# A new order for the first loads and products of a gated attention and token-MLP kernel

## The chip, the cores and the metric

One core of a Trainium2 chip. The metric is the device time of one execution in microseconds (us).

## The reference

The input `x` is 2048 tokens by 512 columns (bfloat16). Two branches are mixed by a gate per token. `a` is attention with 32 heads of 16, where each token sees eight tokens (itself and every second one before it). `b` is an MLP across tokens.

```python
g = sigmoid((x * gate_w).sum(-1, keepdims=True))
# a: sliding dilated attention
q, k, v = split(x @ wqkv)                 # 512 -> 3 x 512, 32 heads of 16
idx = pos[:, None] - 2 * arange(8)        # masked where idx < 0
o = softmax((q . k[idx]) / 4) @ v[idx]
a = o @ wo
# b: token MLP
h = layernorm(x)
u = gelu(einsum("bsd,sf->bdf", h, w1) + b1)   # 2048 tokens -> 1792
b = (einsum("bdf,fs->bds", u, w2) + b2).T     # 1792 -> 2048 tokens
return g * a + (1 - g) * b
```

## The kernel before

The kernel writes down operations with their reads, writes and an estimated duration. A small planner in the same file sorts them into one program per engine: on each engine it takes what can start first by its own estimates, and it sets the semaphores. `after` and the lists given to `chain` fix the order where the author wanted it. On the chip every engine runs its list strictly in order.

Tokens are handled in four blocks of 512. `XT` holds x transposed (columns on partitions, in four slices `dt` of 128 columns), `X` the tokens as they are, for the layernorm and the MLP. A projection (`f_proj`, the matmul at line 619) is four products of 128x128 weights with 128x512 of `XT`, one per slice, summed in one of eight PSUM banks. `tn` is 0, 1 or 2 for q, k and v, `dl` a quarter of their columns, `sb` the block.

**The start.** TensorE runs filler products on constants (`f_warm`, line 537) until data are there. SP first loads the first 128 columns of block 0 as they are (`XP`, `d_xp`). TensorE turns them with the identity (`f_tr`, line 545) into banks 5 and 6; ScalarE copies one half (line 555) and VectorE the other (line 557) into `XT`. The other 384 columns of block 0 come by a transposing DMA (`ld_xt0`, line 473). The first two slices of Wq are loaded on ScalarE's queue. On SP follow, after the transposing DMA, two slices of Wq, four of Wk, x 0 and 1, and block 1's transposing DMA (`ld_xt(1)`, line 460). Later loads wait for an earlier one, five back in the list `init_dmas` (`throttle`). Wv comes in one load of 512 KB behind all blocks of x.

The first 32 real products are q and k of block 0 for all `dl`, in the eight banks, slice by slice as the data come:

```python
for (b0, d0, d1, s0, s1) in ((0, 0, 1, 0, 512), (0, 1, 2, 0, 512), (0, 2, 3, 0, 512),
                             (0, 3, 4, 0, 512), (4, 0, 2, 0, 512), (4, 2, 4, 0, 512)):
    for b in range(b0, b0 + 4):
```

After them comes `seq_proj`: q and k of block 1, q and k of blocks 2 and 3, then v of all blocks. Each group of four products goes to the next of banks 0 to 3, and ScalarE copies it out (lines 627 for q, 630 for k and v).

**What follows.** VectorE forms q times shifted k (`qkm`, line 690): eight half-length products for the first four window positions, four full ones for the rest. TensorE sums them over heads in a burst of 64 products per half (`qkr`, line 698). The softmax, the sums with v (lines 797 to 802) and the layernorm statistics (`ln1`, line 574) are VectorE's too; its order is one long `chain`. The MLP's products are at line 812 (first, followed by the gelu on ScalarE, line 833) and 862 (second, followed by line 930). The output projection is at line 878 and the final mix on VectorE at line 899.

Of the kernel before, what the change touches and what calls it, by code (L numbers as in the profile page):

```python
# [5 lines left out]
BF16 = mybir.dt.bfloat16  # L6
# [3 lines left out]
AF = mybir.ActivationFunctionType  # L10
# [3 lines left out]
D = 512  # L14
# [319 lines left out]
def bass_gated_mix__sliding_local_dilated__mixer_token_mlp__prompt_kernel(nc, A_x, A_wqkv, A_wo, B_x, B_w1, B_b1, B_w2, B_b2, gate_w, out, dbg=None):  # L334
    with contextlib.ExitStack() as es:
        view, pview, off, total = _views(nc, es)
        ps = es.enter_context(nc.psum_tensor("ps", [128, 8, 512], FP32))
        esem = {e: es.enter_context(nc.semaphore("sem_" + e)) for e in ("pool", "act", "dve", "pe")}
        sch = _Sched()

        x2d = A_x[0]
        xv = x2d.rearrange("(t p) d -> p t d", p=128)
        wqkv_v = A_wqkv.rearrange("(dt p) c -> p dt c", p=128)
# [25 lines left out]
        IDENT = view("IDENT", BF16, [(1, 128)])  # L369
# [45 lines left out]
        A = sch.add  # L415
# [12 lines left out]
        def mk_dma(dst, src):  # L428
            return lambda e: e.dma_start(dst, src)

        init_dmas = []
# [4 lines left out]
        def prev_dma():  # L436
            return [init_dmas[-1]] if init_dmas else []

        def ld_x(t0, n, q="sp"):
            ds = sch.dsem("x%d" % t0)  # L440
            op = sch.dma(q, mk_dma(X[:, t0:t0 + n, :], xv[:, t0:t0 + n, :]), n * 128 * D * 2, ds,
                         writes=["x%d" % t for t in range(t0, t0 + n)], deps=throttle() if q == "sp" else [], after=prev_dma() if q == "sp" else [], name="d_x%d" % t0)
            if q == "sp":
                init_dmas.append(op)
            return op

        def ld_w(tn, d0, n, q="sp"):
            ds = sch.dsem("wqkv%d_%d" % (tn, d0))
            op = sch.dma(q, mk_dma(WQKV[:, d0:d0 + n, tn * D:(tn + 1) * D], wqkv_v[:, d0:d0 + n, tn * D:(tn + 1) * D]),
                         n * 128 * D * 2, ds, writes=["wqkv%d_%d" % (tn, dt) for dt in range(d0, d0 + n)],  # L450
                         deps=throttle() if q == "sp" and n == 4 else [], after=prev_dma() if q == "sp" else [],
                         issue=0.65 if n == 4 else 0.45, name="d_wp%d_%d" % (tn, d0))
            if q == "sp":
                init_dmas.append(op)
            return op
# [5 lines left out]
                         writes=["xt_%d" % t for t in range(4 * sb, 4 * sb + 4)], deps=throttle(), after=prev_dma(), name="d_xt%d" % sb)  # L461
            init_dmas.append(op)

        XT0 = ["xt0_%d" % d for d in range(4)] + ["xt0_0b"]
        ALLXT = XT0 + ["xt_%d" % t for t in range(4, NST)]

        def xt_of(sb, d0=0, d1=4):
            return XT0[d0:d1] + (XT0[4:] if d0 == 0 else []) if sb == 0 else ["xt_%d" % t for t in range(4 * sb, 4 * sb + 4)]

        def ld_xt0():  # L470
            ds = sch.dsem("xt0")
            dst = XT[:, 1:4, 0:512]
            op = sch.dma("sp", lambda e: e.dma_start_transpose(dst, x2d[0:512, 128:512]), 512 * 384 * 2, ds, issue=1.25,
                         writes=XT0[1:4], after=prev_dma(), name="d_xt0")
            init_dmas.append(op)
            return op

        XP = view("OUTS", BF16, [(128, 4), (1, 128)])
        d_xp = sch.dma("sp", mk_dma(XP, xv[:, 0:4, 0:128]), 512 * 128 * 2, sch.dsem("xp"), writes=["outs0"], issue=0.4, name="d_xp")
        d_xp.lands = 3.9  # L480
        init_dmas.append(d_xp)

        first_loads = [ld_w(0, 0, 1, "act"), ld_xt0(), ld_w(0, 1, 1, "act"), ld_w(0, 2, 1), ld_w(0, 3, 1), ld_w(1, 0, 2), ld_w(1, 2, 2),
                       ld_x(0, 2)]
        ld_xt(1)
        first_loads.append(init_dmas[-1])
        for op_, t_ in zip(first_loads, (3.5, 5.7, 5.0, 6.3, 6.7, 7.6, 8.6, 9.4, 11.0)):
            op_.lands = t_
            op_.deps.clear()
        first_loads[2].order.add(first_loads[0])  # L490
        init_dmas[:] = [first_loads[1]] + first_loads[5:]
        ld_x(2, 2)
        ld_x(4, 4)
        ld_xt(2)
        ld_xt(3)
        ld_x(8, 4)
        ld_x(12, 4)
        ld_w(2, 0, 4)
        d_w1 = []

        def ld_w1(j):
# [4 lines left out]
            if j < 4:  # L506
# [8 lines left out]
                       writes=["wo"], deps=throttle(), after=prev_dma(), name="d_wo")  # L515
# [25 lines left out]
        def f_tr(h):  # L541
            def fn(e):
                ins = None
                for t in range(2):
                    ins = e.matmul(ps[:, 5 + h, 128 * t:128 * t + 128], lhsT=XP[:, 2 * h + t, :], rhs=IDENT, start=True, stop=True)  # L545
# [5 lines left out]
        ta_ = A("pe", f_tr(0), 0.215, reads=["outs0", "ident"], writes=["lg5_0", "lg5_1"], after=[w2_], name="tr0", prio=-100)  # L551
        tr_ = A("pe", f_tr(1), 0.215, reads=["outs0", "ident"], writes=["lg6_0", "lg6_1"], after=[ta_], name="tr1", prio=-100)
        A("pe", f_warm(1), 0.43, writes=["lg7_0", "lg7_1"], after=[tr_], name="warm3", prio=-100)
        w3_ = tr_
        A("act", lambda e: e.activation(out=XT[:, 0, 0:256], in_=ps[:, 5, 0:256], func=AF.Copy), 0.35, reads=["lg5_0", "lg5_1"],
          writes=["xt0_0"], name="ev_tra", prio=0)
        A("dve", lambda e: e.tensor_copy(out=XT[:, 0, 256:512], in_=ps[:, 6, 0:256]), 0.35, reads=["lg6_0", "lg6_1"],  # L557
          writes=["xt0_0b"], name="ev_trb", prio=0)

        JK = view("OUTS", BF16, [(1, D)], extra=0)  # L560
        def cols(v_, lo, n, step=1):
# [45 lines left out]
        last_main = [None]  # L607
# [37 lines left out]
        seq_proj = []  # L645
        for dl in range(4):
            seq_proj += [(0, dl, 1), (1, dl, 1)]
        for dl in range(4):
            seq_proj += [(0, dl, 2), (0, dl, 3), (1, dl, 2), (1, dl, 3)]
        for dl in range(4):  # L650
            seq_proj += [(2, dl, sb) for sb in range(4)]
        for (tn, dl, sb) in seq_proj:
            xr = xt_of(sb)
            bank = main_bank()
# [1 line left out]
                             reads=xr + ["wqkv%d_%d" % (tn, dt) for dt in range(4)],  # L656
                             writes=["acc%d" % bank], after=[last_main[0]], name="pj_%s%d_%d" % (tnames[tn], dl, sb), prio=0)
# [395 lines left out]
```

## Time and profile before

| | |
|---|---|
| median of 3 runs | 168.34 us (168.12 to 168.81) |
| profiled execution | 168.55 us, span 167.3 us |
| TensorE busy (PE) | 163.9 us, 98% |
| VectorE busy (DVE) | 151.3 us, 90% |
| ScalarE busy (ACT) | 75.0 us, 45% |
| DMA | 29.64 MB, mean 177 GB/s |
| granted TensorE clock | 1.00 |

PE is the matmul part of TensorE and PEld its weight loads, which overlap the matmuls. A row of the timeline gives start, duration, engine, line, operation, shape and count; in square brackets stands how long the engine was idle before it, and what ended that. SPq and ACTq are the queues' issuing instructions. "us to landing" runs from the issue of a DMA until its semaphore is complete. The span leaves out 1.25 us of the profiled execution that lie around it.

### The profile page before, as it was taken

How to read it: one execution, taken by the hardware profiler on the slowest of the kernel's cores; microseconds unless marked ns; L12 is line 12 of the kernel's file. 1: busy time of each engine (PE TensorE's matmuls, PEld its weight loads, DVE VectorE, ACT ScalarE, POOL GpSimd, SP SyncE). 2: the span in 40 equal slices, each digit the busy share in tenths (PEclk: the TensorE clock that was granted, in tenths of full speed). 3: DMA queues.
4: the chain of work that ended last, by engine and by line, in shares of the span. 5: the costliest groups of instructions: out<-in, count | busy, mean ns of one | idle time of the engine just before them, and what ended most of it. 6: DMA issues, size and time to landing. Idle time of an engine off the chain costs nothing.

```text
span 167.3 us, 2152 instructions
## 1 busy us (share of the span) xinstructions
PE 163.9 (98%) x860; PEld 77.6 (46%) x860; DVE 151.3 (90%) x154; ACT 75.0 (45%) x116; POOL 0.7 (0%) x8
## 2 busy tenths in 40 slices
PE   7999999999999999999999999999999999999994
PEld 2455555554454444444444444444444444444463
DVE  0145999999999999999999999999999999999896
ACT  3077688889899818793113121131231321310100
POOL 1000000000000000000000000000000000000000
DMA  5999999968003837996579936462672580000454
GB/s 130 315 272 262 303 322 291 307 196 246 0 0 97 311 115 187 303 290 153 133 183 343 335 129 143 112 187 68 184 218 83 138 223 0 0 0 0 157 190 159
DMA packets 47625, 29.64 MB, mean 177 GB/s; under 512 B 9856, under 2 KB 46464, under 8 KB 47616
## 3 DMA queue, kind: packets, MB, share of 16 engines
q1 hardware_dynamic: 45504, 24.85, 54.0%
q10 hardware_dynamic: 2112, 4.66, 10.0%
q8 instruction: 7, 0.11, 0.3%
q14 instruction: 2, 0.02, 0.0%
HBM read 21.24 MB, written 2.10 MB: 140 GB/s over the span
## 4 chain that ended last, share of the span: by engine, by line
PE 94%; DVE 3%; DMA 2%; issue 0%
PE ps L812 29%; PE ps L862 29%; PE ps L619 25%; PE ps L878 6%; PE ps L698 4%; DVE arena L899 2%; DMA arena<-in_A_x_dram 2%; PE ps L545 0%; DVE arena L557 0%
## 5 line engine op out<-in xcount | busy, mean ns | idle before, releaser
L812 PE MATMUL ps<-arena 128*128 128x512 bf16 x224 | 48.7, 379 | 0.0
L862 PE MATMUL ps<-arena 128*128 128x512 bf16 x224 | 48.7, 379 | 0.0
L619 PE MATMUL ps<-arena 128*128 128x512 bf16 x192 | 42.3, 382 | 0.1
L690 DVE TENSOR_TENSOR arena<-arena 128x4096 bf16<-128x4096 bf16 (+1 forms) x12 | 35.5, 2996 | 2.3 <-ACT arena L630 1.8
L797 DVE TENSOR_TENSOR arena<-arena 128x8192 bf16<-128x8192 bf16 x8 | 35.0, 4419 | 0.0
L812 PEld LDWEIGHTS ps<-arena 128*128 128x128 bf16 x224 | 21.8, 98 | 26.7 <-ACT arena L728 0.4
L862 PEld LDWEIGHTS ps<-arena 128*128 128x128 bf16 x224 | 21.9, 98 | 26.5
L619 PEld LDWEIGHTS ps<-arena 128*128 128x128 bf16 x192 | 21.6, 114 | 20.8 <-DVE arena L557 0.7
L930 ACT ACTIVATE arena<-ps,arena 128x512 bf16<-128x512 f32 x16 | 12.4, 778 | 39.4 <-PE ps L862 39.4
L800 DVE TENSOR_TENSOR arena<-arena 128x4096 bf16<-128x4096 bf16 (+1 forms) x16 | 27.0, 1752 | 0.0
L630 ACT ACTIVATE arena<-ps 128x512 bf16<-128x512 f32 x32 | 18.5, 596 | 4.5 <-PE ps L619 4.5
L833 ACT ACTIVATE arena<-ps,arena 128x512 bf16<-128x512 f32 x14 | 9.6, 687 | 22.2 <-PE ps L812 17.4
L574 DVE BATCH_NORM_STATS2 arena<-arena 128x6 f32<-128x512 bf16 x16 | 10.0, 680 | 5.6 <-DMA arena<-in_A_x_dram 5.6
L878 PE MATMUL ps<-arena 128*128 128x512 bf16 (+1 forms) x80 | 14.2, 337 | 0.0
L899 DVE SCALAR_TENSOR_TENSOR arena<-ps,arena 128x512 bf16<-128x512 f32 (+1 forms) x20 | 11.5, 638 | 0.9 <-PE ps L878 0.7
L598 ACT ACTIVATE arena<-arena 128x512 bf16<-128x512 bf16 x16 | 12.2, 806 | 0.0
L627 ACT ACTIVATE arena<-ps 128x512 bf16<-128x512 f32 x16 | 9.0, 596 | 5.5 <-PE ps L619 5.4
L878 PEld LDWEIGHTS ps<-arena 128*128 128x128 bf16 x80 | 7.8, 98 | 6.3
L674 DVE SCALAR_TENSOR_TENSOR arena<-arena 128x512 bf16<-128x512 bf16 x16 | 10.1, 685 | 0.0
L744 DVE TENSOR_TENSOR arena<-arena 128x512 bf16<-128x512 bf16 (+4 forms) x11 | 7.3, 667 | 0.6 <-ACT arena L763 0.2
L698 PE MATMUL ps<-arena 128*32 128x512 bf16 x128 | 7.3, 380 | 0.0
L728 ACT ACTIVATE arena<-ps 128x512 bf16<-128x512 f32 x8 | 4.7, 592 | 4.6 <-PE ps L698 4.6
(42 smaller groups left out, 40.5 us busy)
## 6 DMA issues: line engine op xcount, KB each, us to landing
arena<-in_B_w_dram SPq DMA_DIRECT2D x7, 1024.0 KB, 8.3
arena<-in_B_w_dram SPq DMA_DIRECT2D x8, 896.0 KB, 5.1
arena<-arena ACTq DMA_DIRECT2D x32, 128.0 KB, 3.0
arena<-in_A_x_dram SPq DMA_DIRECT2D x4, 512.0 KB, 5.1
out_dram<-arena SPq DMA_DIRECT2D x14, 128.0 KB, 1.7
arena<-in_A_x_dram SPq DMA_DIRECT2D x1, 1536.0 KB, 7.9
arena<-in_A_wqkv_dram SPq DMA_DIRECT2D x2, 256.0 KB, 3.6
arena<-in_A_x_dram SPq DMA_DIRECT2D x2, 256.0 KB, 3.5
```

Of the source, the lines that this page charges most:

```text
L598: A("act", (lambda t_: (lambda e: e.activation(out=X[:, t_, :], in_=X[:, t_, :], func=AF.Identity, scale=col(RSTD, t_), bias=col(NMR, t_)) ...
L619: ins = e.matmul(ps[:, bank, s0:s1], lhsT=lhsT, rhs=XT[:, dt, sb * 512 + s0:sb * 512 + s1], start=(dt == 0 and s0 == 0), stop=(dt == 3))
L630: return lambda e: e.activation(out=dst, in_=ps[:, bank, :], func=AF.Copy)
L690: return lambda e: e.tensor_tensor(out=PBL[buf][:, :, 512 * c0:512 * (c0 + nc_)], in0=in0, in1=in1, op=ALU.mult)
L698: ins = e.matmul(ps[32 * c:32 * c + 32, 4 + wl, :], lhsT=RP, rhs=PBL[buf][:, wl, c * 512:(c + 1) * 512], start=(dl == 0), stop=(dl == 3), ...
L797: A("dve", (lambda o_, i0, i1: (lambda e: e.tensor_tensor(out=o_, in0=i0, in1=i1, op=ALU.mult)))(pv, in0, in1), 4.4, reads=v_res + ["atx_% ...
L800: A("dve", (lambda pv_, n__: (lambda e: e.tensor_tensor(out=pv_[:, 0:n__], in0=pv_[:, 0:n__], in1=pv_[:, n__:2 * n__], op=ALU.add)))(pv, n ...
L812: ins = e.matmul(ps[:, bank, :], lhsT=W1W[:, slot, st, 128 * e_:128 * e_ + 128], rhs=X[:, st, :], start=(st == 0), stop=(st == NST - 1))
L862: ins = e.matmul(ps[:, bank, :], lhsT=W2S[slot][:, ft, 128 * e_:128 * e_ + 128], rhs=UT[:, ft, :], start=(ft == 0), stop=(ft == NFT - 1))
L878: ins = e.matmul(ps[:, bank, 0:c1 - c0], lhsT=OT[:, t, 128 * i:128 * i + 128], rhs=WO[:, t, c0:c1], start=(t == 0), stop=(t == 3))
L899: A("dve", (lambda i_, b_, c0_, c1_: (lambda e: e.scalar_tensor_tensor(out=T1[:, i_, c0_:c1_], in0=ps[:, b_, 0:c1_ - c0_], scalar=col(G, i ...
L930: A("act", (lambda i_, bank_: (lambda e: e.activation(out=T1[:, i_, :], in_=ps[:, bank_, :], func=AF.Identity, scale=col(OMG, i_), bias=co ...
```

## The change

- Block 0's first 256 columns, not 128, come as they are: two loads on SP (`ld_xp(0)`, `ld_xp(1)`), each turned by four TensorE products (`turn(0)`, `turn(1)`) and copied by ScalarE and VectorE. The transposing DMA (`ld_xt0`) brings the other 256 columns.
- All first loads are on SP, in one line: columns 0 to 127, Wq slice 0, Wk slice 0, columns 128 to 255, q and k weights of slice 1 in one load (`ld_qk`), the transposing DMA, q and k weights of slices 2 and 3, the whole of Wv, x 0 and 1, then block 1's transposing DMA.
- The filler before the first turn is one product shorter; a half-width one is added after it.
- The first 32 products go q slice 0, the second turn, k slice 0 (banks 4, 7, 5, 6), q and k slice 1, q slice 2, q slice 3, k slices 2 and 3.
- Eight products of v, `dl` 0 and 1 of block 0, stand in front of q and k of block 1.
- In VectorE's chain the copies of both turns come first, and `ln1` 4 and 5 move ahead of the first `qkm`.
- `init_dmas`, the list that later loads throttle on, now starts at the load of slice 2's weights.

```diff
-        XT0 = ["xt0_%d" % d for d in range(4)] + ["xt0_0b"]
+        XT0 = ["xt0_%d" % d for d in range(4)] + ["xt0_0b", "xt0_1b"]
...
-            dst = XT[:, 1:4, 0:512]
-            op = sch.dma("sp", lambda e: e.dma_start_transpose(dst, x2d[0:512, 128:512]), 512 * 384 * 2, ds, issue=1.25,
-                         writes=XT0[1:4], after=prev_dma(), name="d_xt0")
+            dst = XT[:, 2:4, 0:512]
+            op = sch.dma("sp", lambda e: e.dma_start_transpose(dst, x2d[0:512, 256:512]), 512 * 256 * 2, ds, issue=1.25,
+                         writes=XT0[2:4], after=prev_dma(), name="d_xt0")
...
-        XP = view("OUTS", BF16, [(128, 4), (1, 128)])
-        d_xp = sch.dma("sp", mk_dma(XP, xv[:, 0:4, 0:128]), 512 * 128 * 2, sch.dsem("xp"), writes=["outs0"], issue=0.4, name="d_xp")
-        d_xp.lands = 3.9
-        init_dmas.append(d_xp)
-
-        first_loads = [ld_w(0, 0, 1, "act"), ld_xt0(), ld_w(0, 1, 1, "act"), ld_w(0, 2, 1), ld_w(0, 3, 1), ld_w(1, 0, 2), ld_w(1, 2, 2),
-                       ld_x(0, 2)]
+        XP = view("OUTS", BF16, [(512, 2), (128, 4), (1, 128)])
+
+        def ld_xp(dt):
+            op = sch.dma("sp", mk_dma(XP[:, dt], xv[:, 0:4, 128 * dt:128 * dt + 128]), 512 * 128 * 2, sch.dsem("xp%d" % dt),
+                         writes=["outs%d" % dt], after=prev_dma(), issue=0.4, name="d_xp%d" % dt)
...
+        def ld_qk(d):
+            ds = sch.dsem("wqk%d" % d)
+            op = sch.dma("sp", mk_dma(WQKV[:, d, 0:2 * D], wqkv_v[:, d, 0:2 * D]), 2 * 128 * D * 2, ds,
+                         writes=["wqkv0_%d" % d, "wqkv1_%d" % d], after=prev_dma(), issue=0.45, name="d_wqk%d" % d)
...
+        first_loads = [ld_xp(0), ld_w(0, 0, 1), ld_w(1, 0, 1), ld_xp(1), ld_qk(1), ld_xt0(), ld_qk(2), ld_qk(3), ld_w(2, 0, 4), ld_x(0, 2)]
         ld_xt(1)
         first_loads.append(init_dmas[-1])
-        for op_, t_ in zip(first_loads, (3.5, 5.7, 5.0, 6.3, 6.7, 7.6, 8.6, 9.4, 11.0)):
+        for op_, t_ in zip(first_loads, (3.1, 3.8, 4.3, 4.7, 5.8, 7.2, 7.9, 8.6, 10.2, 10.9, 12.8)):
             op_.lands = t_
             op_.deps.clear()
-        first_loads[2].order.add(first_loads[0])
-        init_dmas[:] = [first_loads[1]] + first_loads[5:]
+        init_dmas[:] = first_loads[6:]
...
-        ld_w(2, 0, 4)
...
+        def turn(dt, prev):
+            for h in range(2):
+                lgr = ["lg%d_0" % (5 + h), "lg%d_1" % (5 + h)]
+                prev = A("pe", f_tr(dt, h), 0.215 if dt == 0 else 0.11, reads=["outs%d" % dt, "ident"], writes=lgr, after=[prev],
+                         name="tr%d%d" % (dt, h), prio=-100 if dt == 0 else 0)
...
-        A("pe", f_warm(6), 2.56, writes=["lg7_0", "lg7_1"], name="warm1", prio=-100)
+        A("pe", f_warm(5), 2.13, writes=["lg7_0", "lg7_1"], name="warm1", prio=-100)
         w2_ = A("pe", f_warm(1, 256), 0.2, writes=["lg7_0", "lg7_1"], name="warm2", prio=-100)
...
+        tr_ = turn(0, w2_)
         A("pe", f_warm(1), 0.43, writes=["lg7_0", "lg7_1"], after=[tr_], name="warm3", prio=-100)
...
+        w3_ = A("pe", f_warm(1, 256), 0.2, writes=["lg7_0", "lg7_1"], after=[tr_], name="warm4", prio=-100)
...
-        for (b0, d0, d1, s0, s1) in ((0, 0, 1, 0, 512), (0, 1, 2, 0, 512), (0, 2, 3, 0, 512), (0, 3, 4, 0, 512), (4, 0, 2, 0, 512), (4, 2, 4, 0, 512)):
-            for b in range(b0, b0 + 4):
+        for (bs, d0, d1, s0, s1) in ((range(4), 0, 1, 0, 512), ((4, 7, 5, 6), 0, 1, 0, 512), (range(8), 1, 2, 0, 512),
+                                     (range(4), 2, 3, 0, 512), (range(4), 3, 4, 0, 512), (range(4, 8), 2, 4, 0, 512)):
+            if bs == (4, 7, 5, 6):
+                last_main[0] = turn(1, last_main[0])
+            for b in bs:
...
-        seq_proj = []
+        seq_proj = [(2, dl, 0) for dl in range(2)]
         for dl in range(4):
             seq_proj += [(0, dl, 1), (1, dl, 1)]
...
-            seq_proj += [(2, dl, sb) for sb in range(4)]
+            seq_proj += [(2, dl, sb) for sb in range(1 if dl < 2 else 0, 4)]
...
-        chain(["rp", "ev_trb"] + ln1(0, 1, 2, 3) + ["qkm_0_0_0", "qkm_0_1_0"] + ln1(4, 5, 6, 7) + ln2(0)
+        chain(["rp", "ev_trb0", "ev_trb1"] + ln1(*range(6)) + ["qkm_0_0_0", "qkm_0_1_0"] + ln1(6, 7) + ln2(0)
```

More of the change, by code (lines that the diff above doesn't have):

```diff
@@ L462, in ld_xt @@
             init_dmas.append(op)
-        XT0 = ["xt0_%d" % d for d in range(4)] + ["xt0_0b"]
+        XT0 = ["xt0_%d" % d for d in range(4)] + ["xt0_0b", "xt0_1b"]
         ALLXT = XT0 + ["xt_%d" % t for t in range(4, NST)]
         def xt_of(sb, d0=0, d1=4):
-            return XT0[d0:d1] + (XT0[4:] if d0 == 0 else []) if sb == 0 else ["xt_%d" % t for t in range(4 * sb, 4 * sb + 4)]
+            return XT0[d0:d1] + XT0[4 + d0:4 + d1] if sb == 0 else ["xt_%d" % t for t in range(4 * sb, 4 * sb + 4)]
@@ new lines, in ld_xp @@
+        def ld_xp(dt):
+            op = sch.dma("sp", mk_dma(XP[:, dt], xv[:, 0:4, 128 * dt:128 * dt + 128]), 512 * 128 * 2, sch.dsem("xp%d" % dt),
+                         writes=["outs%d" % dt], after=prev_dma(), issue=0.4, name="d_xp%d" % dt)
+            init_dmas.append(op)
+            return op
+        def ld_qk(d):
+            ds = sch.dsem("wqk%d" % d)
+            op = sch.dma("sp", mk_dma(WQKV[:, d, 0:2 * D], wqkv_v[:, d, 0:2 * D]), 2 * 128 * D * 2, ds,
+                         writes=["wqkv0_%d" % d, "wqkv1_%d" % d], after=prev_dma(), issue=0.45, name="d_wqk%d" % d)
+            init_dmas.append(op)
+            return op
@@ L539, in f_warm, with f_tr @@
             return fn
-        def f_tr(h):
+        def f_tr(dt, h):
             def fn(e):
@@ L544, in fn @@
                 for t in range(2):
-                    ins = e.matmul(ps[:, 5 + h, 128 * t:128 * t + 128], lhsT=XP[:, 2 * h + t, :], rhs=IDENT, start=True, stop=True)
+                    ins = e.matmul(ps[:, 5 + h, 128 * t:128 * t + 128], lhsT=XP[:, dt, 2 * h + t, :], rhs=IDENT, start=True, stop=True)
                 return ins
             return fn
-        A("pe", f_warm(6), 2.56, writes=["lg7_0", "lg7_1"], name="warm1", prio=-100)
+        def turn(dt, prev):
[3 more added lines that the diff above has]
+                         name="tr%d%d" % (dt, h), prio=-100 if dt == 0 else 0)
+                dst = XT[:, dt, 256 * h:256 * h + 256]
+                pin = ps[:, 5 + h, 0:256]
+                if h == 0:
+                    A("act", (lambda d_, i_: (lambda e: e.activation(out=d_, in_=i_, func=AF.Copy)))(dst, pin), 0.35,
+                      reads=lgr, writes=["xt0_%d" % dt], name="ev_tra%d" % dt, prio=0)
+                else:
+                    A("dve", (lambda d_, i_: (lambda e: e.tensor_copy(out=d_, in_=i_)))(dst, pin), 0.35,
+                      reads=lgr, writes=["xt0_%db" % dt], name="ev_trb%d" % dt, prio=0)
+            return prev
@@ L550, in bass_gated_mix__sliding_local_dilated__mixer_token_mlp__prompt_kernel @@
+        A("pe", f_warm(5), 2.13, writes=["lg7_0", "lg7_1"], name="warm1", prio=-100)
         w2_ = A("pe", f_warm(1, 256), 0.2, writes=["lg7_0", "lg7_1"], name="warm2", prio=-100)
-        ta_ = A("pe", f_tr(0), 0.215, reads=["outs0", "ident"], writes=["lg5_0", "lg5_1"], after=[w2_], name="tr0", prio=-100)
-        tr_ = A("pe", f_tr(1), 0.215, reads=["outs0", "ident"], writes=["lg6_0", "lg6_1"], after=[ta_], name="tr1", prio=-100)
+        tr_ = turn(0, w2_)
         A("pe", f_warm(1), 0.43, writes=["lg7_0", "lg7_1"], after=[tr_], name="warm3", prio=-100)
-        w3_ = tr_
@@ L555, in bass_gated_mix__sliding_local_dilated__mixer_token_mlp__prompt_kernel @@
[L555 to L558, printed above, removed]
+        w3_ = A("pe", f_warm(1, 256), 0.2, writes=["lg7_0", "lg7_1"], after=[tr_], name="warm4", prio=-100)
         JK = view("OUTS", BF16, [(1, D)], extra=0)
```

## The prediction

> **What bounds the kernel now.** I read the page's busy times first, then the chain of waits in order of time, then the timeline of the first 22 us, and last the two places where VectorE and TensorE meet.
>
> ```profile
> PE 163.9 (98%) x860; PEld 77.6 (46%) x860; DVE 151.3 (90%) x154; ACT 75.0 (45%) x116; POOL 0.7 (0%) x8
> ```
>
> TensorE has work in 98% of the span, VectorE in 90%. A change to the loads can move the end only through these two engines.
>
> ```profile
> 0.80 3.10 DMA arena<-in_A_x_dram
> 3.91 0.14 issue
> 4.04 0.60 PE ps L545 x4
> 4.64 0.02 issue
> 4.66 0.44 DVE arena L557
> 5.10 0.05 issue
> 5.15 33.44 PE ps L619 x152
> ```
>
> This is the head of the chain of waits. The first load (128 columns of block 0, issued at 0.80) lands at 3.91; TensorE turns it (L545), VectorE copies it (L557), and the first real product starts at 5.15. From there the chain stays on TensorE until 161.65 with no wait between its pieces. So the saving is what the head saves, less what TensorE gets to do on top, unless a new wait opens later.
>
> ```profile
> 5.14 0.15 PEld L619 LDWEIGHTS ps<-arena 128*128 128x128 bf16 x2 [0.68 <-DVE arena L557]
> 5.56 0.15 PEld L619 LDWEIGHTS ps<-arena 128*128 128x128 bf16 x1 [0.27 <-issue]
> 5.98 15.93 PEld L619 LDWEIGHTS ps<-arena 128*128 128x128 bf16 x74 [0.28 <-issue]
> ```
>
> The timeline of the start shows the pace. Weight loads follow the products: 5.14, 5.56, 5.98 is one product per 0.42 us; then 74 in 15.93 us, 0.215 each. The warm-up products before (L537) also step by 0.43. So TensorE runs at half pace until about 6.1, though the granted clock reads 1.00 in this stretch, and three of the real products pay for it: (6.1 - 5.15)/2 = 0.48 us lost.
>
> ```profile
> 15.08 4.49 DVE L690 TENSOR_TENSOR arena<-arena 128x4096 bf16<-128x4096 bf16 x2 [1.84 <-ACT arena L630]
> ...
> 42.20 4.43 DVE L690 TENSOR_TENSOR arena<-arena 128x8192 bf16<-128x8192 bf16 x1 [0.41 <-PE ps L698]
> ```
>
> ```profile
> 157.36 8.29 DVE L899 SCALAR_TENSOR_TENSOR arena<-ps,arena 128x512 bf16<-128x512 f32 x15 [0.72 <-PE ps L878]
> ```
>
> VectorE starts its long chain at 15.08 and then waits for TensorE only in places: 0.41 us at 42.2, 0.72 at 157.36. These are its reserve; a later start costs nothing until they are used up.
>
> **The head, step by step.** Times are of the profiled execution (span 167.3, 168.55 in all, 0.21 above the median 168.34); a difference found there is put on the median.
>
> First load. It keeps its place at 0.80 on SP, but ScalarE's two weight loads (128 KB each, issued 0.80 to 1.82) no longer share the DMA engines with it. At worst it lands at 3.91 as now; at best those 256 KB at some 350 GB/s, the fastest fortieths of the first 12 us, go from ahead of it: 3.91 - 0.75 = 3.16. I take 3.3, nearer the best, because the two loads lie wholly in its time now. Wq's first slice, now second on SP, issues at 1.29 (today's spacing 0.49) and lands 3.0 later, the row of such loads: 4.3. Turning follows landing by 0.13 and the first product follows turning by 1.11 (4.04 to 5.15), so the product starts at 3.3 + 0.13 + 1.11 = 4.54 (4.4 to 5.15). The filler after the turn (four turns 0.43, one wide 0.43, one half 0.21) frees TensorE at 4.50, and Wq is there. Saved: 0.60.
>
> Half pace. If it still ends at 6.1, products now lie under it for 1.56 us and lose 0.78 instead of 0.48: 0.30 given back.
>
> Second turn. Four new 128-column products: 0.107 each at half pace (0.43 in the row of L545 from start to start), 0.055 at full: 0.22 to 0.43. The four products of q ahead take 1.71 at half pace, to 6.2, so I take 0.22. Its data, fourth on SP, issues at 2.3 and lands by 5.4 with today's 3.1: hidden. Banks 5 and 6 are wanted back by k: ScalarE copies in 0.38, VectorE in 0.42, each some 0.2 behind the turn, while TensorE has two k products (0.43) and the second turn itself as cover: 0.1 of wait, at most 0.4.
>
> Sum of the head: -0.60 + 0.30 + 0.22 + 0.10 = +0.02. With the ends of the unknowns, -0.4 to +0.6. The 33rd product, 12.52 now (5.15, three steps to 6.26, 29 of 0.216), stays there.
>
> The pages give a rule against the 256-byte runs: the Trainium skill, "DMA: Bandwidth & Descriptors", Specifications, asks for at least 512 B per transfer for line rate. Here 128 KB in such runs took 3.1 us to land and 128 KB in runs of 1 KB 3.0, so I follow the rows; at half rate the loads behind would come some 0.4 later each, still ahead of their use.
>
> **Behind the head.** The SP order moves: ten loads now stand before block 1's transposing DMA, Wv's 512 KB among them, where seven did on SP. Its issue moves from 5.58 to about 6.4: 0.80, nine plain loads at 0.49, and the smaller transposing one (1.64 x 2/3 = 1.1). At 280 GB/s 512 KB are 1.8 us. Block 1 landed 5.5 us after issue, the median of the three transposing loads of the first 12 us, at 11.0; now 11.0 + 0.9 at least and 11.0 + 0.9 + 1.8 = 13.7 at most. The eight v products end at 12.5 + 8 x 0.216 = 14.2. Those are the cover: no wait, but a margin of only 0.5 at the upper end. Wv itself stands before x 0 and 1, which landed at 9.05, and so lands near 10, before 12.5. x 4 to 7 land at 13.7 now (issue at 9.5, 4.2 to landing), then at 15.5, or 16.4 with the issue delay. ScalarE's issues vanish from 0.80 to 1.82; its table load (1.28) only comes sooner. Nothing there is late.
>
> VectorE. Its first product needs q and k of block 1: 12.5 + 16 x 0.216 + 0.83 (14.25 to 15.08 now) = 16.8, 1.7 later. Two of the bn_stats (0.6 each) go ahead of it, if x 4 has landed by 15.5, and fill 1.2. So VectorE is 0.5 late. The last of its first eight products (L690, start 35.08) then waits for the last k copy, which is 1.73 later too: on ScalarE two such copies ended at 34.90, so 35.8 to 36.6, and the lag there is 0.7 to 1.5. At 42.2 VectorE waits 0.41 for L698's TensorE burst today; that much is absorbed, 0.3 to 1.1 remain. At the softmax the lag reaches ScalarE:
>
> ```profile
> 73.63 2.25 ACT L833 ACTIVATE arena<-ps,arena 128x512 bf16<-128x512 f32 x3
> ```
>
> The first of these three gelus (0.69) frees at 74.32 the bank that the seventh group of the MLP's first product takes at 64.77 + 3 x 3.455 = 75.14. Reserve 0.82. At 157.36 there are 0.72 and some tenths after. A lag up to 0.8 is free, then TensorE stands; I take 0.05 for this. The burst of L698 began at 38.5. The last k product ends at 12.52 + 24 groups of 0.864 = 33.25 now and 1.73 later then, 35.0; four groups are left to 38.5, just enough for copy (0.6), product (2.28) and two hand-overs; 0 to 0.3.
>
> Total: between -0.3 and +0.4 for the likeliest values. The end of half pace need not be at 6.1 in all executions; averaged over earlier ends (below) the head is -0.2, and with 0.05 for VectorE I put -0.15 on the median: 168.2.
>
> **Rivals.**
> The clock, faster. If half pace ended before the first product, today's 0.48 goes and the head saves 0.60 - 0.32 = 0.28: 168.55 - 0.76 = 167.8, and 167.5 with the first load at 3.1. For it: after the turn TensorE stands still for some 0.3 us before 5.15, and the new order fills that; the runs spread from 168.12 to 168.81, about such a stretch. Against: 2.9 us of unbroken warm-up from 0.84 did not end it by 5.1. If it lasts to 7.5 instead, 0.78 becomes 1.48: 169.3. The rule behind it is in the Trainium skill, "TensorE: Matmul & The Clock Gate", Part 1: the window is free-running and about 3.4 us, so an identical kernel meets it at different places. The half pace of the trace agrees; its place in time was seen in one execution only.
>
> Block 1 late, slower. In-order TensorE stands at q of block 1 from 14.2 on, one for one. Landing at 15.1 decides; if Wv's delay is paid twice, once on the SP issue (a transposing load holds SP 3.2 to 3.5 us when the queue is full) and once on the bytes, it lands at 15.3: +1.1, 169.3. For it: the DMA share is over 0.9 in every stretch of 2 us from 2 to 16. Against: 1.4 us beyond my upper end.
>
> VectorE late, slower. A lag of 1.8 at 65 us makes the gelu 1.0 late: 169.3. It needs x 4 to 7 at 17 or L698 two groups later; the 0.41 and 0.82 stand against it.
>
> The eight products of v could also wait for Wv; it would have to land after 12.6, 2.6 late, and I count this with block 1.
>
> **How the numbers follow.** Forecast 0.62 at 168.2 (own range 167.8 to 168.8); clock 0.18, mostly early, about half of it over the bound; block 1 late 0.08; VectorE late 0.12. A difference within 0.5% (0.84 us) is about what a measurement of this kernel cannot tell from none. Faster needs under 167.5: 0.10 from the clock and 0.02 from the forecast. Slower needs over 169.18: most of the two slow rivals and a tail of the forecast and a late clock, 0.18. Same 0.70. Range 167.6 to 169.2.
>
> **What would show it.** First product near 4.5; its step 0.42 until about 6.1; L545 twice with four products; the 33rd product near 12.5; no TensorE wait near 14.2; VectorE's L690 at 16.8 and its wait at 42.2 shorter; TensorE unbroken at 75.1. I am wrong if the first load lands at 3.9, if the half pace ends elsewhere, or if a row of TensorE shows a wait after 12.5.

## The result and the profile after

| | before | after |
|---|---|---|
| median of 22 runs | 168.43 us (167.91 to 168.90) | 169.20 us (168.19 to 170.81) |
| profiled execution | 168.55 us, span 167.3 | 169.48 us, span 168.2 |

The ratio is 1.0042 (95% interval 1.0025 to 1.0058): slower by 0.4%, clear of the noise. The forecast was 168.2, a little faster than before; the median stands at the upper end of the forecast's range, on the other side. One execution of the changed kernel (170.81) was in a slow state and is not in the ratio; without it the runs after still scatter more than twice as wide (168.19 to 170.50).

The chain of waits of the changed kernel, in order of time (start, duration, what), from block 0's transposing DMA on; before these rows it runs over SP's five earlier issues:

```profile
3.34 1.29 SPq L473
4.63 0.05 issue
4.68 0.58 SPq L429
5.26 0.04 issue
5.30 5.39 DMA arena<-in_A_wqkv_dram
10.69 0.05 issue
10.74 29.55 PE ps L636 x136
```

Before, the chain ran through one load that landed at 3.91. Now it runs down SP's issue line to 5.30, through one load of weights (q and k, slice 3) that lands at 10.69, 5.39 us after its issue, and only then reaches TensorE.

Weight loads of TensorE (PEld) at the start; they follow the products:

```profile
4.46 0.15 PEld L636 LDWEIGHTS ps<-arena 128*128 128x128 bf16 x2 [0.57 <-DVE arena L567]
4.88 0.15 PEld L636 LDWEIGHTS ps<-arena 128*128 128x128 bf16 x1 [0.27 <-issue]
5.30 0.15 PEld L636 LDWEIGHTS ps<-arena 128*128 128x128 bf16 x1 [0.28 <-issue]
5.73 0.15 PEld L552 LDWEIGHTS ps<-arena 128*128 128x128 bf16 x1 [0.27 <-issue]
6.16 0.36 PEld L552 LDWEIGHTS ps<-arena 128*128 128x128 bf16 x3 [0.28 <-issue]
...
7.05 2.83 PEld L636 LDWEIGHTS ps<-arena 128*128 128x128 bf16 x14 [0.31 <-ACT arena L564]
10.73 11.37 PEld L636 LDWEIGHTS ps<-arena 128*128 128x128 bf16 x54 [0.86 <-DMA arena<-in_A_wqkv_dram]
```

The first product comes at 4.46, as forecast (4.54). The pace is 0.43 per product until the second turn is over, and the product at 6.58 takes 0.37, so the half pace lasts to 6.9, not 6.1. Twenty products are done by 10.2; then TensorE stands 0.55 us for the weights of slice 3. The 33rd product starts at 13.36; it was 12.52.

VectorE:

```profile
12.91 1.29 DVE L591 BATCH_NORM_STATS2 arena<-arena 128x6 f32<-128x512 bf16 x2 [5.66 <-DMA arena<-in_A_x_dram]
15.69 1.29 DVE L591 BATCH_NORM_STATS2 arena<-arena 128x6 f32<-128x512 bf16 x2 [1.49 <-DMA arena<-in_A_x_dram]
17.46 1.29 DVE L591 BATCH_NORM_STATS2 arena<-arena 128x6 f32<-128x512 bf16 x2 [0.49 <-DMA arena<-in_A_x_dram]
18.66 4.48 DVE L710 TENSOR_TENSOR arena<-arena 128x4096 bf16<-128x4096 bf16 x2
```

Each pair of statistics waits for x; x 4 to 7 land at 17.44 (13.74 before), and VectorE's first attention product starts at 18.66, not at 15.08 and not at the forecast 16.8. Later in the run:

```profile
76.06 1.84 PEld L832 LDWEIGHTS ps<-arena 128*128 128x128 bf16 x10 [0.42 <-ACT arena L853]
```

```profile
154.94 11.65 DVE L919 SCALAR_TENSOR_TENSOR arena<-ps,arena 128x512 bf16<-128x512 f32 x20
```

In the first row TensorE's next weights wait for the gelu (0.10 us between products). In the experiments below this wait stays when VectorE is freed (`after_free`) and goes when the second burst of head sums (L718) is put back (`after_burst`). So it belongs to the burst, which stands four products (0.86 us) later on TensorE's list than before; the prediction had found a reserve of 0.82 there. The second is the final mix: 20 instructions in one piece, where before VectorE waited 0.72 us for TensorE in the middle. The waits at 42 and 157 us that were VectorE's reserve are gone. TensorE and VectorE now reach the end together.

The stages of the start by windows of 2 us (the first row names the columns), the changed kernel first, then the kernel before:

```profile
core 0: us, PE busy (x) PEld busy (x) DVE busy (x) ACT busy (x) POOL busy (x), PEclk, DMA share, GB/s
2.00:4.00 2.00, 1.98 (x9) 0.87 (x8) 0.02 (x1) 0.32 (x2) 0.00 (x0) 1.00 0.83 210
4.00:6.00 2.00, 2.00 (x6) 0.60 (x5) 0.41 (x1) 0.15 (x1) 0.00 (x0) 1.00 1.51 220
6.00:8.00 2.00, 2.00 (x11) 1.11 (x10) 0.42 (x1) 0.38 (x1) 0.00 (x0) 1.00 0.84 221
```

```profile
2.00:4.00 2.00, 1.77 (x5) 0.44 (x3) 0.00 (x0) 1.13 (x1) 0.00 (x0) 1.00 0.94 248
4.00:6.00 2.00, 1.87 (x8) 0.76 (x9) 0.42 (x1) 0.38 (x1) 0.00 (x0) 1.00 1.17 305
6.00:8.00 2.00, 2.00 (x11) 1.04 (x10) 0.00 (x0) 0.00 (x0) 0.00 (x0) 1.00 1.06 313
```

The engines are called busy in both (a share of 1.51 means that packets take long), but fewer bytes move: 0.86 MB against 1.11 by 6 us, 2.9 against 3.4 by 14.

### The profile page after: what moved, and what is told of

The parts are those of the page before. It is cut to its first block, busy times and chain, and to the rows that moved or that the text cites. A ratio compares the mean times of both kernels' runs of the same rounds, so it can differ in the third digit from the quotient of the medians.

```text
span 168.2 us, 2161 instructions
## 1 busy us (share of the span) xinstructions
PE 164.8 (98%) x864; PEld 78.1 (46%) x864; DVE 151.5 (90%) x155; ACT 75.3 (45%) x117; POOL 0.7 (0%) x8
## 4 chain that ended last, share of the span: by engine, by line
PE 90%; DMA 3%; SPq 2%; DVE 2%; issue 0%
PE ps L832 29%; PE ps L882 29%; PE ps L636 22%; PE ps L898 6%; PE ps L718 4%; DMA arena<-in_A_wqkv_dram 3%; DVE arena L919 2%; SPq L429 2%; SPq L473 1%
## 5 line engine op out<-in xcount | busy, mean ns | idle before, releaser
L950 ACT ACTIVATE arena<-ps,arena 128x512 bf16<-128x512 f32 x16 | 12.5, 778 | 39.4 <-PE ps L882 39.4
L898 PE MATMUL ps<-arena 128*128 128x512 bf16 (+1 forms) x80 | 14.2, 336 | 0.0
L718 PE MATMUL ps<-arena 128*32 128x512 bf16 x128 | 7.3, 380 | 0.0
```

The source lines that it names most:

```text
L718: ins = e.matmul(ps[32 * c:32 * c + 32, 4 + wl, :], lhsT=RP, rhs=PBL[buf][:, wl, c * 512:(c + 1) * 512], start=(dl == 0), stop=(dl == 3), ...
L898: ins = e.matmul(ps[:, bank, 0:c1 - c0], lhsT=OT[:, t, 128 * i:128 * i + 128], rhs=WO[:, t, c0:c1], start=(t == 0), stop=(t == 3))
L950: A("act", (lambda i_, bank_: (lambda e: e.activation(out=T1[:, i_, :], in_=ps[:, bank_, :], func=AF.Identity, scale=col(OMG, i_), bias=co ...
```

## One account for all runs

Through all profiles below one sum holds: time = 168.55 + (33rd product - 12.52) + TensorE's waits after it. The 33rd product is the first after q and k of block 0; "later waits" are pauses of TensorE between products after it, beyond those of the kernel before.

| kernel | first product | 33rd | later waits | sum | profiled |
|---|---|---|---|---|---|
| before | 5.15 | 12.52 | 0 | 168.55 | 168.55 |
| before, again | 5.14 | 12.45 | 0 | 168.48 | 168.48 |
| after | 4.46 | 13.36 | 0.10 | 169.49 | 169.48 |
| after, again | 4.46 | 12.33 | 0.10 | 168.46 | 168.52 |
| v_only | 5.13 | 12.49 | 0.10 | 168.62 | 168.61 |
| head_only | 4.29 | 12.94 | 0 | 168.97 | 169.03 |
| q23 | 4.38 | 12.48 | 0.95 + 0.45 | 169.91 | 169.98 |
| noxt | 4.45 | 13.20 | 0.10 | 169.33 | 169.31 |
| v_burst | 5.14 | 12.62 | 0.26 | 168.91 | 168.92 |
| after_burst | 4.35 | 13.11 | 0 | 169.14 | 169.20 |
| v_relief | 5.18 | 12.76 | 0.09 | 168.88 | 168.89 |
| before_relief | 4.97 | 12.12 | 0 | 168.15 | 168.14 |
| v_free | 5.17 | 12.81 | 0.09 | 168.93 | 168.93 |
| after_free | 4.40 | 13.11 | 0.10 | 169.24 | 169.33 |
| head_act | 5.11 | 13.50 | 0 | 169.53 | 169.60 |
| head_xt | 4.37 | 13.69 | 0 | 169.72 | 169.71 |
| v_clear | 5.16 | 12.27 | 0.36 | 168.66 | 168.75 |
| turn1 | 4.41 | 13.54 | 0 | 169.57 | 169.56 |
| wq_sp | 5.04 | 12.16 | 0 | 168.19 | 168.18 |

All agree within 0.1, so in every profiled execution TensorE's list set the time, and VectorE cost something only where it made TensorE wait. The profiled execution is one of many and need not be typical: those of `after_again`, `v_only` and `wq_sp` are among the two fastest of twelve. So the medians and ratios below stand beside it. Each ratio is against the kernel before, run beside the variant on the same chip; the chips differ between experiments, so the ratios compare better than the microseconds.

## The experiments

**The two halves alone.** `v_only` is the kernel before with Wv in front of x 0 and 1, the eight v products, and `ln1` 4 and 5 moved. `head_only` is the changed kernel with these three undone.

```diff
# v_only, on the kernel before
-... ld_w(1, 2, 2), ld_x(0, 2)]
+... ld_w(1, 2, 2), ld_w(2, 0, 4), ld_x(0, 2)]
-        init_dmas[:] = [first_loads[1]] + first_loads[5:]
+        init_dmas[:] = first_loads[5:]
-        seq_proj = []
+        seq_proj = [(2, dl, 0) for dl in range(2)]
```

> The kernel before, with the second half of the change alone: Wv in front of x 0 and 1 and of block 1's transposing DMA, eight products of v in front of q and k of block 1, bn_stats 4 and 5 in front of VectorE's first product. Two-bounds theory (TensorE's head is 0.84 later in the changed kernel, and VectorE starts so late that its reserve is gone; each alone would set the end): here the head stays, 33rd product at 12.5, x 4 to 7 land near 15.3, VectorE's first product at 16.8, its lag of 0.5 is absorbed at 42 and 157 us: 168.4, within 0.2 of before. Rival (the moved v products and Wv cost the time by themselves): 169.0 or more.

Measured: 169.15 us, ratio 1.0040 (1.0018 to 1.0061). The rival was right: this half by itself costs as much as the whole change. Its profiled execution, the fastest of the twelve (168.61), does not show the loss: the head is as before, x 4 to 7 land at 16.08, and TensorE waits 0.10 us at 75. Both bursts of L697 stand four products later on TensorE's list, since the planner, by its own estimates, sees VectorE late.

> The changed kernel with its second half undone: Wv at the end of the loads, v products and bn_stats in the order of before. Two-bounds theory: the head stays late, 33rd product near 13.3, VectorE's first product near 15.9 and its waits at 42 and 157 us are back, the end still late by TensorE alone: 169.1. Rival (VectorE's late start is the cause): 168.4 to 168.5.

Measured: 169.04 us, ratio 1.0025 (1.0004 to 1.0047), as the two-bounds theory has it. The halves cost 0.40% and 0.25%, the whole 0.42%. That fits halves that do not add, each making another engine late, but the intervals leave room for a plain sum. VectorE starts its first product at 15.98 and its wait near the end (0.7 us) is back.

In the profile of `head_only` the waits for the weights of slice 2 (0.15 us between products) and slice 3 (0.50) are there with Wv and the v products back in their old places; 0.14 more goes to block 1's load, which lands at 12.81 in front of the 33rd product:

```profile
8.78 0.58 PEld L637 LDWEIGHTS ps<-arena 128*128 128x128 bf16 x4 [0.43 <-issue]
10.18 2.31 PEld L637 LDWEIGHTS ps<-arena 128*128 128x128 bf16 x12 [0.82 <-DMA arena<-in_A_wqkv_dram]
```

**Other cuts of the weights, and no transposing DMA in block 0.**

```diff
# q23, on the changed kernel
-... ld_xt0(), ld_qk(2), ld_qk(3), ...
+... ld_xt0(), ld_w(0, 2, 2), ld_w(1, 2, 2), ...
# noxt, on the changed kernel: columns 128 to 511 plain, in one load; other banks for the turns
-first_loads = [ld_xp(0), ld_w(0, 0, 1), ld_w(1, 0, 1), ld_xp(1), ld_qk(1), ld_xt0(), ld_qk(2), ...
+first_loads = [ld_xp(0), ld_w(0, 0, 1), ld_xp(1), ld_w(1, 0, 1), ld_qk(1), ld_qk(2), ...
+                for dt_ in (1, 2, 3):
+                    last_main[0] = turn(dt_, last_main[0])
```

> The changed kernel; the two loads of q and k weights of slices 2 and 3 are cut the other way, q of both slices first, then k of both, in rows of 1 KB in place of 2 KB. The products of q on slice 3 then wait only for the first of the two. Two-bounds theory: TensorE's wait of 0.55 at 10.2 goes, 33rd product near 12.8, but VectorE still starts at 18.6, TensorE waits 0.4 to 0.6 more near 75 us: 169.1, gain 0.1 at most. Rival (the wait for the weights is the whole cause): 168.6.

Measured: 169.16 us, ratio 1.0038 (1.0021 to 1.0054), as the two-bounds theory said. But the profile, of the longest execution of the twelve, shows more than it did: 0.55 is still waited from 8.5, for the first of the two loads, and TensorE then stands 0.95 us from 14.2 for block 1, whose transposing DMA lands at 15.02, and 0.45 at 76.1. Here the 33rd product came at 12.48, and the next load in line was late.

```profile
12.37 1.51 PEld L636 LDWEIGHTS ps<-arena 128*128 128x128 bf16 x8 [0.21 <-ACT arena L644]
15.12 0.80 PEld L636 LDWEIGHTS ps<-arena 128*128 128x128 bf16 x5 [1.24 <-ACT arena L647]
```

The second row names ScalarE for this wait; what fits the time is block 1's DMA, which landed 0.1 us before it ended.

> The changed kernel without a transposing DMA in block 0: all 512 columns come as they are in two plain loads (128 and 384 columns) and are turned on TensorE, twelve turns where the second turn had four. Theory of the stop (engines that reach the transposing DMA stand until the slowest has finished the plain loads before it: 0.8 to 1.2 us from 5.5 to 6.7): that stop goes, the weights of slice 3 land by 8.5, x 4 to 7 near 16.2, VectorE's first product near 17.6, 33rd product near 13.2 with 0.45 for the turns: 168.9. Rival (the DMA engines are only full): slice 3's weights near 10.5 as now, the same wait, and with the turns 169.6.

Measured: 169.22 us, ratio 1.0048 (1.0031 to 1.0066). Slice 3's weights land at 9.19 instead of 10.69 and no product waits for them, x 4 to 7 land at 16.5: the way the theory of the stop has it, though the weights come 0.7 us later than it said. The twelve turns and their copies take about 1.1 us, so the 33rd product is at 13.20 all the same. The time lies between the two forecasts, 0.3 above the first and 0.4 below the second.

**VectorE and the second burst.** `v_burst` and `after_burst` put the second burst of head sums back, with one line:

```diff
+        byname["ph2_3_0"].order.add(byname["qkr_1_3"])
```

`v_relief` and `before_relief` shorten gate sums, `v_free` and `after_free` bn_stats as well, `v_clear` is `v_free` with the line above:

```diff
+            if 3 <= t < 12:
+                src, gw = XA[:, t, 0:64], GWB[:, 0:64]
...
-in_=X[:, t_, :]
+in_=X[:, t_, 0:D if t_ < 4 else 64]
```

> The kernel with the second half of the change alone, and the second burst of head sums (64 products) put back in front of the MLP's seventh group of products, where it stood before; the new plan had set it four products later. Theory 1 (the late burst starts VectorE's softmax 0.86 late and with the late loads uses up VectorE's reserve of 1.2): the wait at 75 us goes, VectorE waits 0.5 to 0.7 near 157 us again, 168.5 to 168.7. Theory 2 (the time is lost in the head, by waits for loads that come late in most executions): unchanged, 169.1.

Measured: 169.06 us, ratio 1.0044 (1.0025 to 1.0063). The burst's place is not the cause of the loss; theory 1 falls in this form. In the profile x 4 to 7 land at 16.86, VectorE starts at 18.09, and the wait at 75 us is 0.26.

> The changed kernel with the same burst put back in front of the seventh group. Theory 1: the wait at 75 us goes, but TensorE's own head is 0.4 to 0.8 late and stays: 168.9 to 169.1. Theory 2: unchanged or, as q and k reach VectorE late, 0.3 of waiting at the burst: 169.2 to 169.5.

Measured: 169.48 us, ratio 1.0070 (1.0046 to 1.0095). No gain, as theory 2 had it. In the profile the wait at 75 us is gone, but TensorE stands 1.28 us for slice 2's weights, which land at 9.38:

```profile
6.47 1.45 PEld L636 LDWEIGHTS ps<-arena 128*128 128x128 bf16 x8 [0.16 <-DMA arena<-in_A_wqkv_dram]
9.48 0.58 PEld L636 LDWEIGHTS ps<-arena 128*128 128x128 bf16 x4 [1.57 <-issue]
```

> The kernel with the second half of the change alone, with VectorE relieved: the nine gate sums for tokens 384 to 1535 run over 64 of the 512 columns, so the gate's value is not the reference's there. This takes some 4.5 us from VectorE after 69 us and none before. Theory 1: VectorE no longer sets the end, only the wait at 75 us (0.1 or more) stays: 168.5 to 168.8. Theory 2: 169.1, as without relief.

Measured: 168.89 us, ratio 1.0052 (1.0031 to 1.0073). No gain that can be told, which speaks against a loss by VectorE's work after 69 us. The profile shows VectorE waiting 3.6 us for TensorE at the final mix.

> The kernel before with the same relief of VectorE (gate sums of tokens 384 to 1535 over 64 of 512 columns). Theory 1: VectorE had 1.2 us of reserve, TensorE sets the end: 168.4 to 168.5, no difference. Theory 2: the same. If it is faster by more than 0.2, VectorE set the end before the change too, in many executions.

Measured: 168.41 us, ratio 1.0007 (0.9993 to 1.0021). Before the change VectorE's work after 69 us did not set the end.

> The kernel with the second half of the change alone, VectorE relieved early and late: bn_stats of tokens 512 to 2047 and gate sums of tokens 384 to 1535 run over 64 of 512 columns, so layernorm and gate there are not the reference's. Some 5 us go from VectorE before 42 us, another 4.5 after 69. Theory V (VectorE's late start costs the time: by the wait of the gelu at 75 us and by its own end): 168.3 to 168.5, no wait of TensorE at 75. Theory H (TensorE's own head costs it): 168.9 to 169.1 as without relief.

Measured: 168.73 us, ratio 1.0014 (0.9998 to 1.0031). The time lies between the two forecasts; by the ratio most of the second half's cost is gone once VectorE is relieved early too. The intervals of `v_only` and `v_free` overlap, but the three variants with an unrelieved early VectorE stand at 1.0040 to 1.0052 and the two with a relieved one (this and the next) at 1.0013 and 1.0014. So VectorE's lag from the late start is the likely cause; no profile of this half shows TensorE waiting more than 0.26 us at 75 us. The 0.09 us of waiting at 75 us stays here, with VectorE free, and is gone in the next variant: that part is the burst's place.

> The second half of the change alone, VectorE relieved early and late as before (bn_stats of tokens 512 to 2047 and gate sums of tokens 384 to 1535 over 64 of 512 columns, layernorm and gate there not the reference's), and the second burst of head sums put back in front of the MLP's seventh group. If VectorE's lag and the late burst together are all that the second half costs: no wait of TensorE at 75 us, 168.3 to 168.45, the time of before. If its loads delay TensorE's head too: 33rd product later than 12.5 in most executions, 168.7 as with the relief alone.

Measured: 168.65 us, ratio 1.0013 (0.9992 to 1.0033): not told apart from `v_free`, nor from before. In this profile TensorE waits 0.36 us from 14.0 for block 1 (landing at 14.22).

> The changed kernel with the same early and late relief of VectorE. Theory V with a late head: what is left is TensorE's head, as in the first half of the change alone, 168.8 to 169.0. If all were VectorE: 168.4. If VectorE played no part: 169.2 to 169.5.

Measured: 169.47 us, ratio 1.0067 (1.0045 to 1.0089). In the whole change VectorE can be freed without a gain. That is the forecast for a VectorE that plays no part, not that of theory V. The 33rd product is at 13.11, after waits of 0.55 for slice 2's weights (landing at 9.37) and 0.12 for slice 3's. It also lies above `head_only` (1.0025): what Wv and the v products add to the head beyond VectorE was not tried by itself.

**The head's parts.**

```diff
# head_act, on head_only
-first_loads = [ld_xp(0), ld_w(0, 0, 1), ld_w(1, 0, 1), ld_xp(1), ...
+first_loads = [ld_xp(0), ld_w(0, 0, 1, "act"), ld_w(1, 0, 1, "act"), ld_xp(1), ...
# head_xt, on head_only
-... ld_w(1, 0, 1), ld_xp(1), ld_qk(1), ld_xt0(), ld_qk(2), ...
+... ld_w(1, 0, 1), ld_xt0(), ld_xp(1), ld_qk(1), ld_qk(2), ...
# turn1, on head_only: 128 plain columns, transposing DMA of 384, no second turn
+... ld_w(1, 0, 1), ld_xt0(), ld_qk(1), ld_qk(2), ...
```

> The first half of the change alone, with the first slices of Wq and Wk issued on ScalarE's queue again, beside SP. The loads of SP move up by 1 us. If the one line of SP costs the time: weights of slice 3 land near 9.3, the wait of 0.5 goes, 168.5. If the DMA engines and their stop at the transposing DMA cost it: first load 0.5 later (3.6 to 3.9), the stop stays, 168.9 to 169.2.

Measured: 170.15 us, ratio 1.0102 (1.0076 to 1.0129), the slowest. The first load lands at 3.87 again, so all the gain is gone and the second turn stays. In the profile (169.60) the half pace lasts to 7.7 and nothing waits for weights; what the longer executions wait for was not seen.

> The first half of the change alone, with block 0's transposing DMA moved two places up, in front of the second plain 128 columns and the 256 KB load of slice 1's weights. If engines that reach the transposing DMA stand until the slowest has finished the plain loads before it, the stop shrinks from 1 us to under 0.4, slice 3's weights land before 9.5, no wait for them, 33rd product 12.4 to 12.7: 168.4 to 168.6. If the stop does not hang on what stands before: as the first half alone, 169.0.

Measured: 169.69 us, ratio 1.0080 (1.0057 to 1.0103). The longest packet of block 0's transposing DMA took 0.38 us, as the first theory said, and slice 3's weights landed at 9.83 without a wait. But the second plain columns, now behind it, land at 6.87 where TensorE is free for them by 6.1, and slice 1's weights at 8.44. These waits cost 0.9 and 0.35 us.

> The first half of the change alone, without the second turn: one plain load of 128 columns, a transposing DMA of 384, fourth on SP's one line. If the turn costs what it takes (0.22 to 0.43) and nothing else changes: 168.6 to 168.7. If TensorE then waits for the larger transposing DMA and the weights behind it (landing near 6.8 and 7.5 against 6.2 wanted): 168.8 to 169.2.

Measured: 169.56 us, ratio 1.0077 (1.0050 to 1.0105), worse than either forecast.

```profile
4.41 1.44 PEld L637 LDWEIGHTS ps<-arena 128*128 128x128 bf16 x8 [0.57 <-DVE arena L568]
8.33 5.76 PEld L637 LDWEIGHTS ps<-arena 128*128 128x128 bf16 x28 [2.48 <-issue]
```

Here the half pace ended before the second product; eight products were done by 6.2, and TensorE stood 2.2 us for slice 1's weights (landed at 8.23, behind the transposing DMA). An earlier and faster TensorE only waited longer in this run.

**The same programs again.**

> The changed kernel once more, on this chip. The end of the half pace is not tied to the program: it lies anywhere from 4.5 to 7.5, and the time follows the 33rd product: 168.55 + (33rd product - 12.52) + the waits after it, within 0.2. Rival (the change itself sets it): half pace ends at 6.9 again.

Measured: 169.22 us, ratio 1.0050 (1.0027 to 1.0072); its profiled execution took 168.52, one us less than the first.

```profile
5.30 0.15 PEld L636 LDWEIGHTS ps<-arena 128*128 128x128 bf16 x1 [0.28 <-issue]
5.72 0.43 PEld L552 LDWEIGHTS ps<-arena 128*128 128x128 bf16 x4 [0.28 <-DMA arena<-in_A_x_dram]
6.11 0.17 PEld L636 LDWEIGHTS ps<-arena 128*128 128x128 bf16 x2
6.68 1.87 PEld L636 LDWEIGHTS ps<-arena 128*128 128x128 bf16 x10 [0.41 <-ACT arena L564]
8.73 5.23 PEld L636 LDWEIGHTS ps<-arena 128*128 128x128 bf16 x25 [0.17 <-issue]
```

The half pace ends at 5.7, when the fourth product starts, the turns step by 0.056 in place of 0.107, slice 3's weights land at 9.28 and nothing waits for them; the banks cost 0.12 us. The two terms close the difference between the profiles: 0.58 from the half pace and 0.58 from the weights, less the 0.12. So the head that was forecast does occur, in the second fastest of these twelve executions; the median stayed at 169.22.

> The kernel before once more, with a profile. If the end of the half pace is not tied to the program, it differs from 6.1 by some tenths or more and the time moves by half of that. Rival: 6.1 again within 0.1.

Measured: 168.48 us; half pace to 5.97, 0.07 less loss, 0.07 us less time. A shift of 0.14 lies between the two forecasts and decides nothing; the ends at 6.9 and 5.7 in the two executions of the changed kernel do.

**What of it could be kept.** `wq_sp` is the kernel before with only the first slice of Wq moved from ScalarE's queue to SP's second place.

```diff
-first_loads = [ld_w(0, 0, 1, "act"), ld_xt0(), ...
+first_loads = [ld_w(0, 0, 1), ld_xt0(), ...
```

> The kernel before, with one load moved: the first slice of Wq is issued on SP behind the first plain load, in place of ScalarE's queue; all else as before. If the early first product is worth half of what it gains and nothing else is lost: first load lands 3.5, first product 4.75, 33rd product 0.2 earlier than before, 168.2 to 168.3. If the half microsecond by which SP's other loads move back turns into a wait for slice 1: 168.5 to 168.8.

Measured: 168.59 us, ratio 1.0012 (1.0001 to 1.0022). In the profile, the fastest of the twelve (168.18), the first load landed at 3.80, 0.1 earlier only, with the other load of ScalarE still beside it; slice 1 cost under 0.05 us, but block 1's load, at 12.03, cost 0.14 us. The median has the size of the second forecast, without its mechanism in the profile. No version was found that beats the kernel before.

## Why the prediction was wrong

**Right.** The first load (landing 3.22 against 3.3), the first product (4.46 against 4.54), the second turn's data hidden behind q, at most 0.12 of waiting at banks 5 and 6 (0.1 allowed), and that TensorE's list decides.

**Right by luck.** That no product waits for block 1. In the first profile its load landed at 14.67, beyond the 13.7 that the prediction put as the most (in the second at 13.39). From the forecast 33rd product, 12.5, the eight v products would have ended at 14.2 and TensorE would have stood 0.4 us; they covered the load only because the head was late itself. In `q23` and `v_clear`, whose heads were not late, TensorE did wait, 0.95 and 0.36 us. Wv landed at 12.06, not near 10. This is the rival "Block 1 late", which had a chance of 0.08.

**Failed: "Behind the head", a term that was missing.** The sum had no landing for the q and k weights of slices 2 and 3. They stand behind block 0's transposing DMA on SP's one line, which issues at 3.34 where it was 1.29. The last of them landed at 10.69 and cost 0.55 us, 0.58 with a short pause behind it; before, the last Wk landed at 8.39, 2.4 us ahead of its first product. Of the six profiles with this order of loads (`after`, `after_again`, `head_only`, `after_burst`, `after_free`, and `q23`, which cuts these weights the other way) five wait for these weights, for 0.55 to 1.4 us, and `after_again` does not. "Nothing there is late" was said of Wv, x and block 1 only, and by a rate of 280 GB/s that the new order did not keep (220 from 4 to 8 us, 246 from 4 to 14).

**Mis-sized: the half pace.** 0.30 was given back in the sum; in the first profile it was 0.72, because half pace ended at 6.9. The total of the head closes with these two: -0.68 (first product) + 0.72 + 0.22 (turn) + 0.58 = +0.84, against +0.02. The prediction took the end of the half pace for a rival, and faster at that. Over the 19 profiles it lies between 4.1 or earlier (`before_relief`, whose first turn already runs at full pace) and 7.7 (`head_act`). This agrees with the Trainium skill, "TensorE: Matmul & The Clock Gate", Part 1, which lets the window of 3.4 us run free; the two executions of the changed kernel show it for one program (6.9 and 5.7). Neither end is a gain of the change: an earlier start at half pace returns half of it.

**Mis-sized: x 4 to 7.** Forecast 15.5 to 16.4, measured 17.44, 16.05 in the second profile, 16.1 to 17.4 in the variants of the second half. VectorE's lag was set at 0.5 by it; it was 18.66 - 15.08 - 1.21 = 2.4 here and 1.0 to 1.8 with the old head. That is the mechanism of the rival "VectorE late", which had a chance of 0.12 and needed x 4 to 7 at 17. Its places were named rightly: the waits at 42 and 157 us vanish and the gelu at 75 us stops TensorE, for 0.1 to 0.45; of this 0.1 belongs to the burst, which stands one group later (the rival asked for two).

**The two sums were made one after the other.** The forecast charged 0.05 for VectorE because it took TensorE for the bound and x 4 to 7 for early. `head_only` (0.25%) and `v_only` (0.40%) show that each half costs time by itself. For the whole change the profiles show the head's cost term by term; that VectorE's lag is a second bound beside it is argued from `v_free` and not shown.

**Still open.** What the longer executions of `head_act` and of `v_only` wait for; why `after_free` and `after_burst` stand above the changed kernel's other runs, if they do; and how the second half's remaining 0.1%, if it is any, falls on block 1's load and the burst.

## What to carry to other kernels

When loads are put in one line, price the landing of every one against the instruction that needs it, not only of the first and of those that were moved; the chain of waits before the change shows none of those that had room. When two engines are busy for 98% and 90% of the span, list the waits of the second as its reserve, and charge a later start against them before calling it free. An earlier first product is worth only what the next loads in line let it be: of the profiles that began at 4.5 or earlier, all but `after_again` and `noxt` then waited for a load, and `noxt` paid for twelve turns.

## What the runs showed of the hardware

Packets of a transposing DMA stood for long behind plain loads. In the changed kernel 19 packets of 256 bytes of block 1's transposing DMA, which take 0.018 us as a rule, took about 1.3 us, all ending near 12.6. The plain load of Wv in front had landed in pieces: the 16 increments of its semaphore, which I read as one per DMA engine, came from 10.61 to 12.06. Block 0's packets stood in the same way from 5.5 to 6.7.

How long they stood differs between executions. The longest packet of block 1's load took 0.48 us in the first profile of the kernel before; 1.05 to 2.09 us in ten of the eleven profiles with Wv in front, and 0.56 in the eleventh, `after_again`. Without Wv in front it took 0.46 to 1.22 us (1.22 in `before_relief`, which loads as the kernel before does), so Wv is not the only source. At block 0 it took 0.56 to 1.21 us behind the 256 KB of slice 1 and 0.1 to 0.4 without; with no transposing DMA there (`noxt`) no such packet stood.

Behind Wv the longest packet goes with the spread of Wv's landing: 0.67 us of spread and 0.56 in `after_again`, 1.45 and 1.34 in the changed kernel, 2.16 and 2.09 in `q23`. This fits engines that wait for the slowest one; which load makes an engine slow was not tried by itself. One program had 1.47 us between the first and last increment at slice 3's weights in one execution and 0.74 in the other.
